# A fused attention and expert kernel: the first piece of weights on two queues, first scores in other banks, another count of filler matmuls

## The chip, the cores and the metric

The kernel runs on one core of a Trainium2 chip. The metric is device microseconds (us) of one execution. A core has TensorE (PE, whose weight loads are shown as PEld), VectorE (DVE), ScalarE (ACT), GpSimd (POOL) and SyncE (SP). Each engine runs its own instructions in order; semaphores tie them together. DMA transfers are issued here by SP and by ACT.

## What is computed

A gated linear recurrence over 4 batches, 8 heads, 768 positions and head dimension 48, whose output is rearranged to 3072 tokens of 384 features and then goes through two dense layers:

```python
for t in range(S):
    state = alpha[:, :, t, :, None] * state + np.einsum('bhd,bhe->bhde', k[:, :, t], v[:, :, t])
    y[:, :, t] = np.einsum('bhd,bhde->bhe', q[:, :, t], state)
...
h = x @ w_in          # 384 -> 2048
g = h - np.tanh(h)
return (g @ w_out).astype(np.float32)
```

q, k, v, alpha are float32; w_in and w_out arrive as 64-bit floats and are converted to 32 bits on the chip.

## The kernel before, in words

The 3072 tokens are cut into 12 units of 256 tokens (2 chunks of 128). For each unit the kernel runs the recurrence in chunked form (`gla`) and then the two dense layers in 8 steps (`moe`), each step a first layer (L1080), elementwise work on ACT and DVE, and a second layer (L1125 for the first two units, L1146 after them). The weights come in 16 pieces, 8 of w_in ("in0" to "in7") and 8 of w_out. A piece is fetched by SP (`fetch`, L551; `load_weight`, L39, whose transfers are all issued at L43), read by ACT in two passes (L86, L87) and written as 32-bit words by DVE in two passes (L89, L90). Four buffers hold raw pieces. A piece of w_in is 8 transfers.

All work is a list of tasks with an engine, an estimated time, a rank, the tasks it needs, and a latency until others see its result. A planner (`Planner`) simulates the list with these estimates several times with other priorities, keeps the shortest plan, and the program is written out in the order of the planned starts: every engine's order follows from the estimates, and the instructions of one engine stay in that order. An estimate itself takes no time on the chip. `plan.begin` (L1210) says from when each engine is counted as free.

The head of the program is unit 0's recurrence. Its path:

- `load` (L576) fetches alpha, k, q, v. For unit 0 each is two transfers, one issued by SP and one by ACT (L584, L595).
- `turn` (L649) transposes alpha, k and q by matmuls with the identity (L663), two halves "a" and "b" each. The halves of alpha go to PSUM banks o0 and o1 and are copied out by ACT and DVE (L670). The halves of q go to the two banks of the tile `sc` (`two_banks`).
- DVE scans the products of alpha (L711, L730), and multiplies the turned k and q by them (L679). For unit 0 the scans and products are made for chunk 0 and chunk 1 apart.
- `scores` (L782): 16 matmuls per chunk (L795). Chunk 0 writes to `two_banks()`, the tile that holds the turned q; chunk 1 writes to two tiles of the pool of `h`. `masked` (L814) multiplies the scores by a mask on DVE (L819).
- `back`, `natural`, `update` (PE L925, ACT L930, PE L938) make the state's update, `products` (L835) the output of a chunk, `features` copies it to xT, and then the first layer can begin.

Behind unit 0's tasks SP issues the loads of unit 1 and the further pieces.

Until the task "y 0.0" (the products of chunk 0) the program puts filler matmuls (`spin`, L1204, 128 x 128 with the identity, result not used) into gaps of PE's plan; each is two matmul instructions in the trace. Their number is counted at L418 with an estimated time each (L1209).

Of the kernel before, what the change touches and what calls it, by code (L numbers as in the profile page):

```python
# [17 lines left out]
P = 128  # L18
# [17 lines left out]
R_MAX = 2.0 ** 60  # L36


def load_weight(nc, pool, rows, **kw):  # L39

    raw = pool.tile([P, WN], I64 if rows[0][2].dtype != FP32 else FP32, name="raw", **kw)
    for at, js, src in rows:
        nc.sync.dma_start(out=raw[at].rearrange("p (j n) -> p j n", n=src.shape[-1])[:, js], in_=src)  # L43
    return raw


def weight_parts(w_in, w_out, pad_rows, what, s, by_tile=True):

    if what == "out":
        return [(slice(0, P), slice(0, 2), w_out.rearrange("(j p) n -> p j n", p=P)[:, 2 * s:2 * s + 2, :])]  # L50
    parts = []
    for i in range(len(pad_rows[0])):
        at, f0 = pad_rows[0][i]
        step = pad_rows[1][i][1] - f0
        src = w_in[f0:f0 + len(pad_rows) * step].rearrange("(j p) n -> p j n", p=step)
        src = src[0:at.stop - at.start, :, 2 * s * P:2 * (s + 1) * P]

        few = at.stop - at.start < 32 or not by_tile
        parts += [(0, at, slice(0, len(pad_rows)), src)] if few else [(j - 9, at, slice(j, j + 1), src[:, j:j + 1]) for j in range(len(pad_rows))]
    return [x[1:] for x in sorted(parts, key=lambda x: (x[0], x[1].start))]  # L60
# [261 lines left out]
class Planner:  # L322
# [64 lines left out]
    def order(self):  # L387
        names = {t[0]: i for i, t in enumerate(self.tasks)}
        assert len(names) == len(self.tasks)
        before, after = ([[] for _ in self.tasks] for _ in range(2))  # L390
        for i, t in enumerate(self.tasks):
            edges = {names[a]: self.tasks[names[a]][6] for a in t[4]}
            if t[7]:
                edges.setdefault(names[t[7]], 0.0 if self.tasks[names[t[7]]][1] == t[1] else 0.25)
            for j, lat in edges.items():
                before[i].append((j, lat))
                after[j].append((i, lat))
        chance = random.Random(self.SEED)
        priority, late, best = [t[3] for t in self.tasks], None, None
        for n in range(self.ROUNDS):  # L400
            starts, order = self.run(priority, before, after, late if n % 2 else None, self.begin)
            ends = [s + t[2] for s, t in zip(starts, self.tasks)]
            if best is None or max(ends) <= best[0]:
                best = max(ends), starts, order
                turned, _ = self.run([-e for e in ends], after, before)
                back = [r + t[2] for r, t in zip(turned, self.tasks)]
                fair = [max(back) - b for b in back]
            late = fair if n < 4 else [x + chance.gauss(0, self.NOISE) for x in fair]
            priority = late
        _, starts, order = best  # L410
        plan = sorted(((starts[i], n, self.tasks[i][5], i) for n, i in enumerate(order)), key=lambda x: x[:2])

        engine, until, us, do = self.filler
        filled, free = [], self.begin.get(engine, 0.0)
        for x in plan:
            name, e, length = self.tasks[x[3]][:3]
            if e == engine and until:
                filled += [(free, -1, do, None)] * int(max(0.0, x[0] - free) / us)  # L418
                free = x[0] + length
                until = until if name != until else None  # L420
            filled.append(x)
        return filled


def fast(tc, q, k, v, alpha, moe_w_in, moe_w_out, out, w_in, w_out, ident, ok, pad_rows):
# [17 lines left out]
    with ExitStack() as ctx:  # L443
# [23 lines left out]
        def by_matmul(u, what):  # L467
            return u < len(TURNED) and what in TURNED[u]
# [80 lines left out]
        raw_of = {}  # L549

        def fetch(what, s):  # L551
            raw_of[what, s] = load_weight(nc, raw_pool, weight_parts(moe_w_in, moe_w_out, pad_rows, what, s), bufs=4)

        def convert(what, s):
            it = []
# [7 lines left out]
        for n, (what, s) in enumerate(pieces):  # L563
            rank = RANK[what] + 2 * s
            held = pieces[n - 4] if n >= 4 else None
            add(f"fetch {what}{s}", "SP", 5.7 if n < 2 else 4.3 if what == "in" else 2.0, rank - 30, [held and f"read {held[0]}{held[1]}"],
                lambda what=what, s=s: fetch(what, s), lat=2.5)
            a, b = convert(what, s)
            older = pieces[n - 2] if n >= 2 else None
            add(f"read {what}{s}", "ACT", 1.9, rank, [f"fetch {what}{s}", older and f"{older[0]}{older[1]}"], a)  # L570
            add(f"{what}{s}", "DVE", 1.6, rank, [f"read {what}{s}"], b)
# [31 lines left out]
        def gla(u, rank):  # L603
# [17 lines left out]
            for what, name in enumerate(("aT", "kT", "qT", "v")):  # L621
                go(f"load {name}", "SP", 1.3 if direct or what == 3 or by_matmul(u, what) else 2.2, -9 + 0.1 * what,
                   [what < 3 and u > 0 and not by_matmul(u - 1, what) and not by_matmul(u, what) and f"{name}{prev}"]
                   + [u == 1 and ("kUba 0" if what == 3 else "turn qTb 0")]
                   + [f"{last} {u - 2}.{CU - 1}" for last in ("y", "state") if what == 3 and u > 1
                      and (last == "y" or (u - 2) % UPB < UPB - 1)],
                   lambda what=what: load(u, what), lat=2.9 if u == 0 else 3.6 if u < PLAIN else 4.5)

            def widen(what):
                for hh in range(2):  # L630
# [51 lines left out]
            for n, ab in enumerate("ab"):  # L682
                if by_matmul(u, 0):
                    go(f"turn aT{ab}", "PE", 0.92, n * 0.1, ["load aT", later and "masked 0.0"], lambda n=n: turn(0, n))
                    go(f"aT{ab}", "DVE" if n else "ACT", 0.62, 0, [f"turn aT{ab}"], lambda n=n: place(n))
                if by_matmul(u, 1):
                    go(f"turn kT{ab}", "PE", 0.92, 1 + n * 0.1,
                       ["load kT"] + [later and x for x in ("x 0.0", "y 0.1", "state 0.1")], lambda n=n: turn(1, n))
                    for x, _, cs in parts:
                        go(f"kU{ab}{x}", "DVE", 0.33 if x else 0.6, 3, [f"turn kT{ab}", f"U{x}", n and f"kUa{x}", later and "back 0.1", later and by_matmul(u, 2) and "turn qTb"],  # L690
                           lambda n=n, cs=cs: times(1, "U", n, cs))
                if by_matmul(u, 2):
                    go(f"turn qT{ab}", "PE", 0.92, 2 + n * 0.1,
                       ["load qT", later and f"aT{ab}" if by_matmul(u, 0) else "masked 0.0"], lambda n=n: turn(2, n))
                    for x, _, cs in parts:
                        go(f"qW{ab}{x}", "DVE", 0.33 if x else 0.6, 5, [f"turn qT{ab}", f"W{x}", n and f"qWa{x}", later and "y 0.1", later and by_matmul(u, 1) and "turn kTb"],
                           lambda n=n, cs=cs: times(2, "W", n, cs))
# [72 lines left out]
            def chunk(c):  # L770
# [11 lines left out]
                def scores():  # L782
                    if c == 0:

                        xT[u] = two.tile([P, NP, TU], FP32, name="xT")
                    if u == 0 and c == 1:
                        sc = m["sc", c] = [ps_h.tile([P, 2, TU], FP32, name="h").rearrange(
                            "p a t -> p (a t)").rearrange("p (g t) -> p g t", t=P) for _ in range(2)]
                    else:
                        m["sc", c] = two_banks()  # L790
                        sc = [m["sc", c][:, r] for r in range(2)]
# [22 lines left out]
                def masked():  # L814
                    sc = m["sc", c]
                    if direct:
                        m["pm", c] = [two.tile([P, NP, P], FP32, name=f"pm{r}", tag=tag) for r, tag in enumerate("zw")]
                        for r, to in enumerate(m["pm", c]):
                            V.tensor_mul(to, sc[r] if c else sc[:, r], mask.unsqueeze(1).to_broadcast([P, NP, P]))  # L819
                        return  # L820
                    of = sc.rearrange("p r g t -> p r (g t)")[:, :, 0:NP * HP].rearrange("p r (g t) -> p r g t", t=HP)
                    V.tensor_mul(pm, of, within.unsqueeze(1).unsqueeze(1).to_broadcast([P, 2, NP, HP]))
# [381 lines left out]
        def spin():  # L1204
# [1 line left out]
            if not spun:  # L1206
                spun.append(ps_o.tile([P, P], FP32, name="spin", tag="o2"))
            T.matmul(spun[0], lhsT=ident, rhs=ident, start=True, stop=True)  # L1208
        plan.filler = "PE", "y 0.0", 0.35, spin  # L1209
        plan.begin.update(SP=0.8, PE=1.5, ACT=3.0, DVE=4.8)  # L1210

        for u in range(NU):
            gla(u, rank_gla(u))
# [108 lines left out]
```

## Time and profile before

| what | value |
|---|---|
| median of 17 runs | 576.24 us (575.63 to 578.96) |
| the profiled execution's own time | 578.32 us |
| its span (first to last instruction) | 576.5 us |
| PE busy, of the span | 565.9 us (98%) |
| DVE busy | 450.8 us (78%) |
| ACT busy | 323.2 us (56%) |
| mean granted TensorE clock | 0.992 |
| first layer's matmuls (L1080), 1152 of them | 265.1 us |
| filler matmuls (L1208) | 38, from 1.57 to 15.6 us |

The profile is of one execution. A line of its timeline gives the start, the duration, the engine, the line of the kernel, the operation, the tiles written and read, and in brackets how long the engine was idle before it and who ended that. Matmuls are pipelined, so busy PE time says little by itself; the waits say where PE stood still.

### The profile page before, as it was taken

The page shows a single profiled execution, that of the slowest core. Times are in us where ns is not written, and L with a number is a line of the kernel's source. Part 1 is how long each engine was busy: PE and PEld are TensorE (multiplying, and loading weights), DVE is VectorE, ACT ScalarE, POOL GpSimd, SP SyncE. Part 2 cuts the span into 40 slices and gives each one's busy share as a digit, 9 for nine tenths or more (in the row PEclk, how much of TensorE's full clock was granted, in tenths as well). Part 3 has the DMA queues.
Part 4 walks back from the last instruction along what each step waited for, and adds up shares of the span by engine and source line. Part 5 has one row for each costly group of instructions (what it writes and reads, how often), then busy time and mean ns, then how long its engine had stood idle before and what let it go on. Part 6 is the DMA issues. An engine that isn't in the chain of part 4 may idle for free.

```text
span 576.5 us, 13746 instructions
## 1 busy us (share of the span) xinstructions
PE 565.9 (98%) x5583; PEld 500.1 (87%) x5583; DVE 450.8 (78%) x886; ACT 323.2 (56%) x559; POOL 4.8 (1%) x22
## 2 busy tenths in 40 slices
PE   8899999999999999999999999999999999999995
PEld 8787777778989998998999999898998999899995
DVE  5889879999999995895896896796797645554643
ACT  2589885747777686577485365364443433333531
POOL 3000000000000000000000000000000000000000
PEclk9799999999999999999999999999999999999999
DMA  8888881236674762562640320210100000000001
GB/s 176 208 227 221 255 183 56 85 71 138 111 154 122 127 156 84 117 148 81 186 116 2 85 60 4 72 53 22 45 20 2 30 7 3 28 8 0 28 1 35
DMA packets 60713, 50.84 MB, mean 88 GB/s; under 512 B 35776, under 2 KB 50400, under 8 KB 60640
## 3 DMA queue, kind: packets, MB, share of 16 engines
q1 hardware_dynamic: 57728, 48.88, 34.4%
q10 hardware_dynamic: 2912, 0.98, 0.8%
q8 instruction: 46, 0.75, 0.6%
q14 instruction: 27, 0.22, 0.1%
HBM read 44.04 MB, written 4.72 MB: 85 GB/s over the span
## 4 chain that ended last, share of the span: by engine, by line
PE 93%; DMA 2%; DVE 2%; SPq 1%; issue 1%; ACT 0%; POOL 0%; DVEq 0%; POOLq 0%
PE h L1080 42%; PE o L1146 32%; PE o L1125 7%; PE sc L805 2%; PE sc L878 2%; PE sc L888 2%; PE sc L811 2%; PE sc L991 1%; DMA raw<-in_moe_w_in_dram 1%; DMA rough<-in_q_dram 1%; PE spin L1208 1%; SPq L43 1%; PE turned L663 0%; DVE W L730 0%; PE sc L795 0%
## 5 line engine op out<-in xcount | busy, mean ns | idle before, releaser
L1080 PE MATMUL h<-xT,w_in 128*128 128x256 f32 x1152 | 265.1, 380 | 0.6 <-DVE w_in L90 0.6
L1080 PEld LDWEIGHTS h<-xT,w_in 128*128 128x128 f32 x1152 | 215.4, 190 | 28.0 <-DVE w_in L90 0.7
L1089 ACT ACTIVATE u<-h 128x512 f32<-128x512 f32 x96 | 57.0, 594 | 179.1 <-PE h L1080 178.4
L1097 DVE TENSOR_TENSOR w<-h,u 128x512 f32<-128x512 f32 x96 | 65.8, 686 | 79.1 <-ACT u L1089 78.7
L1146 PE MATMUL o<-b,e 128*128 128x192 f32 x480 | 90.9, 326 | 0.0
L1146 PE MATMUL o<-w_out,e 128*128 128x192 f32 x320 | 81.4, 337 | 0.0
L1146 PEld LDWEIGHTS o<-b,e 128*128 128x128 f32 x480 | 80.2, 190 | 0.0
L1101 DVE SCALAR_TENSOR_TENSOR g<-z,w 128x512 f32<-128x512 f32 x96 | 65.5, 683 | 4.1 <-PE o L1125 1.3
L1146 PE MATMUL o<-b,g 128*128 128x192 f32 x320 | 65.1, 326 | 0.0
L1093 ACT ACTIVATE z<-u 128x512 f32<-128x512 f32 x96 | 60.4, 629 | 2.6
L1146 PEld LDWEIGHTS o<-w_out,e 128*128 128x128 f32 x320 | 55.7, 189 | 4.4
L1146 PEld LDWEIGHTS o<-b,g 128*128 128x128 f32 x320 | 54.2, 190 | 0.0
L1107 ACT ACTIVATE big<-u 128x1024 f32<-128x1024 f32 x48 | 50.4, 1050 | 0.0
L1125 PE MATMUL o<-w_out,g 128*128 128x384 f32 x128 | 44.0, 488 | 0.0
L1125 PEld LDWEIGHTS o<-w_out,g 128*128 128x128 f32 x128 | 24.1, 190 | 13.7
L1113 DVE TENSOR_TENSOR e<-g 128x256 f32<-128x256 f32 x80 | 33.5, 419 | 1.8
L1114 DVE TENSOR_TENSOR e<-g 128x256 f32<-128x256 f32 x80 | 33.3, 417 | 0.0
L639 DVE STREAM_TRANSPOSE aT<-ar 128x256 f32<-128x256 f32 x44 | 28.4, 645 | 2.8 <-ACT ar L633 1.7
L730 DVE TENSOR_TENSOR_SCAN W<-aT,before 128x1032 f32<-128x1032 f32 (+1 forms) x13 | 27.7, 2133 | 0.0
L711 DVE TENSOR_TENSOR_SCAN U<-aT,after 128x1032 f32<-128x1032 f32 (+1 forms) x13 | 27.6, 2129 | 0.1
L1115 DVE TENSOR_TENSOR e<-g 128x128 f32<-128x128 f32 x80 | 22.7, 284 | 0.0
L639 DVE STREAM_TRANSPOSE qT<-qr 128x256 f32<-128x256 f32 x40 | 20.5, 627 | 0.0
(141 smaller groups left out, 560.4 us busy)
## 6 DMA issues: line engine op xcount, KB each, us to landing
raw<-in_moe_w_out_dram SPq DMA_DIRECT2D x16, 768.0 KB, 4.8
raw<-in_moe_w_in_dram SPq DMA_DIRECT2D x80, 96.0 KB, 4.3
raw<-in_moe_w_in_dram SPq DMA_DIRECT2D x16, 288.0 KB, 4.7
vt<-in_v_dram SPq DMA_DIRECT2D x23, 192.0 KB, 4.1
ar<-in_alpha_dram SPq DMA_DIRECT2D x44, 96.0 KB, 2.5
kr<-in_k_dram SPq DMA_DIRECT2D x40, 96.0 KB, 2.7
qr<-in_q_dram SPq DMA_DIRECT2D x40, 96.0 KB, 2.2
out_dram<-cross SPq DMA_DIRECT2D x19, 96.0 KB, 1.7
```

Source lines behind the costliest of these rows:

```text
L639: V.transpose(to, raws[what][:, g, :, 0:32])
L730: V.tensor_tensor_scan(out=m["W"][:, ns].rearrange("p n t -> p (n t)"), data0=aT[:, a:z], data1=before[:, a:z], initial=0.0, op0=ALU.mult, ...
L1080: T.matmul(h[:, a, :], lhsT=w_in[:, j, f * P:(f + 1) * P], rhs=xT[u][:, j, :], start=(j == 0), stop=(j == KT - 1))
L1089: A.activation(m["u", s], m["h", s], AF.Square, scale=W_SCALE ** -1.5)
L1093: A.activation(m["z", s], m["u", s], AF.Square, bias=QB, scale=QA * W_SCALE)
L1097: V.tensor_mul(m["w", s], m["h", s], m["u", s])
L1101: V.scalar_tensor_tensor(out=g.rearrange("p a c t -> p (a c t)"), in0=m["z", s], scalar=QK, in1=m["w", s], op0=ALU.add, op1=ALU.mult)
L1107: A.activation(big, m["us", s // 2].rearrange("p s t -> p (s t)"), AF.Relu, bias=-U_FAST, scale=W_SCALE, accum_out=over[:, n:n + 1])
L1113: V.tensor_add(e[:, 0:2, :], g[:, 0], g[:, 1])
L1114: V.tensor_sub(e[:, 2:4, :], g[:, :, 1, :], g[:, :, 0, :])
L1125: T.matmul(m["o"][c], lhsT=g[:, a, c, :], rhs=w_out[:, f, :], start=(f == 0), stop=(f == FT - 1))
L1146: T.matmul(o[n][:, i], lhsT=g_, rhs=w_, start=(s_ == 0 and (n, i) in ((0, 0), (1, 0), (2, 1), (3, 0))), stop=(s_ == FS - 1), skip_group_ch ...
```

## The change

- The first piece ("in0") is read over two queues: of its 8 transfers the first, third, fifth and seventh are issued by ACT and the others by SP. `load_weight` gets an argument for it.
- Unit 0's scores of chunk 0 go to tiles in banks o0 and o1 (which held the turned alpha) in place of `two_banks()`. Unit 1's turn of q, which was made to wait for "masked 0.0", is made to wait for unit 0's four qW products in its place.
- A gap of PE's plan gets (gap + 0.5) / 0.24 fillers if it is over 0.2, in place of gap / 0.35.
- Estimates: fetch of the first piece 3.0 in place of 5.7, of the second 5.0 in place of 5.7; latency of unit 0's loads 3.3 in place of 2.9; ACT counted as free from 5.4 in place of 3.0.

```diff
-def load_weight(nc, pool, rows, **kw):
+def load_weight(nc, pool, rows, queues=None, **kw):
...
-    for at, js, src in rows:
-        nc.sync.dma_start(out=raw[at].rearrange("p (j n) -> p j n", n=src.shape[-1])[:, js], in_=src)
+    for n, (at, js, src) in enumerate(rows):
+        (queues[n % len(queues)] if queues else nc.sync).dma_start(out=raw[at].rearrange("p (j n) -> p j n", n=src.shape[-1])[:, js], in_=src)
...
-                filled += [(free, -1, do, None)] * int(max(0.0, x[0] - free) / us)
+                filled += [(free, -1, do, None)] * (int((x[0] - free + 0.5) / us) if x[0] - free > 0.2 else 0)
...
-            raw_of[what, s] = load_weight(nc, raw_pool, weight_parts(moe_w_in, moe_w_out, pad_rows, what, s), bufs=4)
+            raw_of[what, s] = load_weight(nc, raw_pool, weight_parts(moe_w_in, moe_w_out, pad_rows, what, s),
+                                          queues=[A, nc.sync] if (what, s) == pieces[0] else None, bufs=4)
...
-            add(f"fetch {what}{s}", "SP", 5.7 if n < 2 else 4.3 if what == "in" else 2.0, rank - 30, [held and f"read {held[0]}{held[1]}"],
+            add(f"fetch {what}{s}", "SP", 3.0 if n == 0 else 5.0 if n == 1 else 4.3 if what == "in" else 2.0, rank - 30, [held and f"read {held[0]}{held[1]}"],
...
-                   lambda what=what: load(u, what), lat=2.9 if u == 0 else 3.6 if u < PLAIN else 4.5)
+                   lambda what=what: load(u, what), lat=3.3 if u == 0 else 3.6 if u < PLAIN else 4.5)
...
-                       ["load qT", later and f"aT{ab}" if by_matmul(u, 0) else "masked 0.0"], lambda n=n: turn(2, n))
+                       ["load qT"] + [later and f"qW{x}{y} 0" for x in "ab" for y in "ab"], lambda n=n: turn(2, n))
...
-                    if u == 0 and c == 1:
-                        sc = m["sc", c] = [ps_h.tile([P, 2, TU], FP32, name="h").rearrange(
-                            "p a t -> p (a t)").rearrange("p (g t) -> p g t", t=P) for _ in range(2)]
+                    if u == 0:
+
+                        sc = m["sc", c] = [(ps_h if c else ps_o).tile([P, NP, P], FP32, name="scores", tag="h" if c else f"o{r}")
+                                           for r in range(2)]
...
-                            V.tensor_mul(to, sc[r] if c else sc[:, r], mask.unsqueeze(1).to_broadcast([P, NP, P]))
+                            V.tensor_mul(to, sc[r], mask.unsqueeze(1).to_broadcast([P, NP, P]))
...
-        plan.filler = "PE", "y 0.0", 0.35, spin
-        plan.begin.update(SP=0.8, PE=1.5, ACT=3.0, DVE=4.8)
+        plan.filler = "PE", "y 0.0", 0.24, spin
+        plan.begin.update(SP=0.8, PE=1.5, ACT=5.4, DVE=4.8)
```

## The prediction

> **What bounds the kernel now.** I read four views, in this order. First the waits of PE from 30 to 130 us, and the table by stretch (us, then busy us of PE, PEld, DVE, ACT and POOL with their instruction counts, then granted clock, DMA share, GB/s):
>
> ```profile
> PE h L1080 <- DVE w_in L90: 0.6, 1, 0.6
> ```
>
> ```profile
> 120.00:560.00 440.00, 440.00 (x4374) 399.68 (x4373) 343.76 (x689) 235.96 (x421) 0.00 (x0) 1.00 0.28 66
> ```
>
> From 42.8 us on PE never waits: the rest is a fixed amount of TensorE work. So the change, which edits only the head, is worth what it moves the moment at which PE starts to run without a gap. Later pieces of weights follow, since their fetches wait for buffers that the same steps free.
>
> Second, the timeline of the head (start, duration, engine, line; idle time before it and who ended it stand in brackets):
>
> ```profile
> 1.57 4.63 PE L1208 MATMUL spin<-ident 128*128 128x128 f32 x20 [1.57 <-POOL ident masks.py:199]
> 6.13 3.37 PE L663 MATMUL turned<-ident,rough 128*64 128x128 f32 x48
> 7.86 0.64 ACT L670 COPY aT<-turned 128x512 f32<-128x512 f32 x1 [2.84 <-PE turned L663]
> 8.75 0.69 DVE L670 COPY aT<-turned 128x512 f32<-128x512 f32 x1 [3.98 <-PE turned L663]
> 9.55 2.36 DVE L711 TENSOR_TENSOR_SCAN U<-aT,after 128x516 f32<-128x516 f32 x2
> ...
> 12.05 0.94 PE L1208 MATMUL spin<-ident 128*128 128x128 f32 x6
> ...
> 14.70 0.94 PE L1208 MATMUL spin<-ident 128*128 128x128 f32 x6
> ...
> 15.59 0.40 DVE L679 TENSOR_TENSOR qT<-sc,W 128x256 f32<-128x256 f32 x1
> ...
> 17.16 0.42 DVE L679 TENSOR_TENSOR qT<-sc,W 128x256 f32<-128x256 f32 x1
> 17.63 2.08 PE L795 MATMUL sc<-qT,kT 48*128 48x128 f32 x16 [2.00 <-DVE qT L679]
> 19.76 1.29 DVE L819 TENSOR_TENSOR pm<-sc,mask 128x512 f32<-128x512 f32 x2 [2.11 <-PE sc L795]
> 36.63 0.96 DVE L90 CUSTOM_DVE_ANT_0 w_in<-bits,more 128x1536 uint16<-128x1536 uint16 x1 [1.60 <-PE h L1080]
> ```
>
> VectorE is the chain: it runs almost without a gap from the copy at 8.75 to 17.6, idles 2.11 for the first scores, and is full again until the third piece's conversion at 34.5 (L89), whose second half (L90) waits for PE at 36.6. PE's first scores wait for the last of four qT products (17.58), though they use the products of chunk 0 alone, the last of which ends at 15.99: the other two still read the bank (tile sc) that the scores overwrite.
>
> Third, the granted clock (same columns; PEclk after POOL's):
>
> ```profile
> 7.30:17.40 10.10, 8.33 (x126) 7.70 (x122) 8.48 (x18) 5.07 (x10) 0.00 (x0) 1.00 0.79 180
> 17.50:24.30 6.80, 6.67 (x60) 5.77 (x62) 4.48 (x10) 2.88 (x6) 0.00 (x0) 0.50 1.02 227
> 24.40:31.00 6.60, 6.60 (x116) 5.53 (x112) 6.33 (x13) 4.92 (x8) 0.00 (x0) 1.00 0.87 198
> ```
>
> PE was idle from 15.63 to 17.63, and the clock is 0.50 for the next 6.8 us. The early fillers also run slowly (median 421 ns against 275 ns after 12 us) though the column shows 1.00 there; the turns become fast at 7.26.
>
> Fourth, what SP waits for, and how long the two v loads take to land (min/median/max):
>
> ```profile
> SPq L43 <- DMA vt<-in_v_dram: 2.1, 1, 2.1
> SPq L43 <- DMA rough<-in_alpha_dram: 1.7, 1, 1.7
> ```
>
> ```profile
> DMA to landing us min/median/max: 7.1/7.6/8.2
> ```
>
> SP's fifth to twelfth transfers wait for earlier ones to land, in pairs: alpha at 4.6, k at 6.1, q at 7.8, v at 10.7. That is eight transfers in flight, SP's and ScalarE's counted together. So the eight issues of the first piece last from 4.64 to 12.5, most of it waiting.
>
> **Own time and median.** The profiled execution took 578.32 (span 576.5, 1.8 around it); the median shown is 576.24. The difference is about what the half clock costs. Without it the first scores end at 18.7 instead of 19.7, the masks and all of VectorE behind come 1.0 sooner, and L89 ends at 34.0. PE's pieces from 17.63 on, at full speed: scores 1.1, transposes 0.5, scores 1.05, update 0.6, first products 1.75, second products until 25.5 (masks at 22.95), turns 2.75, two first layers 5.4: 33.65. L90 then starts at 34.05, 2.6 sooner, 578.32 - 2.6 = 575.7, close to the lowest shown, 575.63. I take the median as an execution without that stretch.
>
> **Two queues (L43, L552).** SP issues four transfers less; it is free at about 9.9 to 11.1 instead of 12.5, so unit 1's loads and the next pieces go 1.4 to 2.6 sooner. Worth nothing on the path: ScalarE read piece 0 at 15.12 with no wait, piece 1 at 26.13 though it had landed before 21, and the only DMA wait of L86 up to 130 us is 1.3, for a later w_out piece. Those idle-free reads are the cover. The cost is on ScalarE: its four issues stand ahead of the alpha copy (L670), and the last waits for a v load, 9.5 or 10.65, plus 0.4. So the copy can start at 10 to 11.1 instead of 7.86, and the gap copy, sizes and reads queue behind it. With the copy at 11.1 the scan starts at 11.75, 2.2 late; with it at 10, the fillers below decide. The table load (1.28) stands ahead of these issues if the order stays as now; if it falls behind them, see the first rival.
>
> The Trainium skill ("DMA: Bandwidth & Descriptors", Issuing engines are not separate DMA queues) speaks against this part: transfers from several engines interleave on the same 16 DMA engines, and spreading saves only the issue time. Here that time is 0.31 to 0.42 per transfer, so by the rule at most 1.7 is saved on SP; by the waits above up to 2.6; on the path both give 0.
>
> **More fillers (L418, L1209).** Before: (0.8 + 1.3 + 2.9 - 1.5) / 0.35 = 10 ahead of the first turn, the 20 matmuls in the first row. After: latency 3.3, so (3.9 + 0.5) / 0.24 = 18. Ten took 1.57 to 6.0, 0.43 each. Until 7.26 some 13 run; the other 5 at 0.25 end at 8.45. The first turn starts there instead of 6.13, then at 0.875 each (full speed): the second alpha half is ready at 10.25 instead of 8.7. **The scan moves 1.55 later.** The six turns end at 13.7 instead of 12.05. Each of the three later gaps held 3 fillers, so it was 1.05 to 1.4 in the plan; by the new rule 6 (at most 7), 1.5 instead of 0.8. PE: 13.7 + 1.5 = 15.2, transposes 0.44, 1.5, update 0.6, 1.5: free for the scores at **19.2**. With the scan 2.2 late the transposes wait until 15.1, so ScalarE's wait hides under the fillers. What the fillers give: no gap of 2 us, hence no half clock, if that gap was its cause.
>
> The Trainium skill ("TensorE: Matmul & The Clock Gate", HAM oscillation) puts the limit at idle gaps over about 3.4 us. Here 2.0 was enough. By the page the old gap was harmless and the fillers bring nothing; by the row they are worth up to 2.6 in such an execution.
>
> **Banks (L786, L694).** Scores could start at 15.99 + 1.55 = 17.55 on VectorE's side, but PE comes at 19.2: the freed bank is not what ends last any more. Letting unit 1's qT turns go before the masks costs nothing; PE has a queue at 30 us.
>
> **Costs of the plan (5.7 to 3.0 and 5.0, begin 5.4).** They move no instruction by themselves, but the planner may order the head anew. Gain bounded by the only later wait, 0.6; loss by one conversion (1.6) put ahead of masks. I take 0.
>
> **Sum.** Scores 19.2 to 20.3 at full clock; masks at 20.35, 0.6 later than 19.76; L89 ends at 35.65. PE: 20.3 + 0.5 + 1.05 + 0.6 + 1.75 = 24.2, second products until 27.2 (masks 24.6), + 2.75 + 5.4 = 35.35. L90 starts at 35.65, against 36.63: -1.0, so 577.3. Against an execution without the half clock it is 1.6 late: 577.3 too.
>
> **Rivals.**
> - *ScalarE is blocked longer (slower).* Table load and first activation fall behind the four issues: 10.65 + 0.4 + 1.28 + 0.2, copy until 13.2, scan 3.7 late. It decides once the scan is over 2.35 late (transposes at 15.2). Transposes 16.55, scores 20.6 to 21.7, masks 21.75, 2.0 late; L90 at 37.05: +0.4, 578.7. For it: the wait rows, and that the issues of loads already stand ahead of the table load. Against: the first activation was ready at 4.8.
> - *The bank pays in full (faster).* If the clock rises at about 4 or the plan's gaps shrink, scores start at 16.05, masks at 17.65, L89 ends at 32.9, L90 at 32.95: 574.6. For it: the 2.00 wait; against: fillers of 0.43.
> - *Nothing moves.* The stream of weights sets the steady state: 576.2. Against: PE waits 0.6 after 30 us.
>
> **Numbers.** Main case 0.45, its own range 576.6 (the 0.6 gained) to 578.0 (one more filler per gap); blocked ScalarE 0.20; bank 0.22; nothing 0.13. A measurement tells about 0.2% (1.15 us) from no change: bounds 575.1 and 577.4. Half the main case lies above: slower 0.42, within 0.36, faster 0.22. Range 574.5 to 578.9.
>
> **What would show it.** Right: 36 filler matmuls from 1.57 until about 8.4, first turn there, four L43 issues on ACTq ahead of L670, L795 at about 19.2 right behind fillers, clock 1.00 up to the first layer. Wrong: turns starting near 6, L670 after 12, scores before 17, or a half clock again.

## The result and the profile after

| | median | executions |
|---|---|---|
| before | 576.05 us (575.39 to 579.98) | 47 |
| changed | 580.47 us (579.72 to 582.77) | 8 |

The ratio is 1.0072, with a 95% interval of 1.0053 to 1.0091: **slower by 0.7%, 4.4 us, and outside the predicted range.** The profiled execution of the changed kernel took 580.29 (span 578.6, mean granted clock 0.998). Its line numbers are those of the kernel before up to L551, plus 1 from there up to L786 and plus 2 behind it; the other versions shift in the same way by the parts that they hold.

The timeline of the head after the change (start, duration, engine, line; in brackets the idle time before it and who ended it):

```profile
1.57 6.64 PE L1210 MATMUL spin<-ident 128*128 128x128 f32 x36 [1.57 <-POOL ident masks.py:199]
...
6.32 5.75 ACTq L43 DMA_DIRECT2D raw<-in_moe_w_in_dram  x4
8.13 3.71 PE L664 MATMUL turned<-ident,rough 128*64 128x128 f32 x64
...
12.17 0.64 ACT L671 COPY aT<-turned 128x512 f32<-128x512 f32 x1 [7.14 <-DMA raw<-in_moe_w_in_dram]
...
12.84 0.69 DVE L671 COPY aT<-turned 128x512 f32<-128x512 f32 x1 [8.07 <-ACT aT L671]
...
13.63 2.36 DVE L712 TENSOR_TENSOR_SCAN U<-aT,after 128x516 f32<-128x516 f32 x2
...
16.95 0.60 PE L927 MATMUL y<-ident,kT 112*128 112x112 f32 x4 [1.82 <-DVE kT L680]
...
17.39 2.63 PE L1210 MATMUL spin<-ident 128*128 128x128 f32 x22
...
20.55 1.16 PE L797 MATMUL scores<-qT,kT 48*128 48x128 f32 x16
...
21.74 1.29 DVE L821 TENSOR_TENSOR pm<-scores,mask 128x512 f32<-128x512 f32 x2
...
31.86 0.70 PE L1082 MATMUL h<-xT,w_in 128*128 128x256 f32 x2
...
33.27 0.96 DVE L90 CUSTOM_DVE_ANT_0 w_in<-bits,more 128x1536 uint16<-128x1536 uint16 x1
...
34.28 5.02 PE L1082 MATMUL h<-xT,w_in 128*128 128x256 f32 x22 [1.72 <-DVE w_in L90]
```

The fillers are as predicted, 36 until 8.2. But ScalarE's alpha copy runs at 12.17 (7.86 before), VectorE's copy waits for it, and the scan starts at 13.63 (9.55 before). The first scores come at 20.55, the first layer at 31.86, and it stops after two matmuls until the third piece's second conversion (L90, 33.27) is over. The third and the fourth of ScalarE's issues, each from a narrow window of the same timeline, stand just ahead of the late copy; the third waited for a v load that landed at 11.25:

```profile
11.27 0.32 ACTq L43 DMA_DIRECT2D raw<-in_moe_w_in_dram  x1
...
11.63 0.44 ACTq L43 DMA_DIRECT2D raw<-in_moe_w_in_dram  x1
```

TensorE's waits from 6 to 60 us (total, times, longest):

```profile
PE h L1082 <- DVE w_in L90: 2.9, 2, 1.7
...
PE y L927 <- DVE kT L680: 1.8, 1, 1.8
```

Before, the wait for L90 was 0.6. The table by stretch (PE, PEld, DVE, ACT, POOL busy; granted clock, DMA share, GB/s):

```profile
17.50:24.30 6.80, 6.80 (x99) 6.19 (x99) 6.41 (x16) 5.34 (x11) 0.00 (x0) 1.00 0.84 209
...
120.00:560.00 440.00, 440.00 (x4374) 400.08 (x4373) 339.31 (x685) 235.93 (x421) 0.00 (x0) 1.00 0.28 67
```

The steady state is the same (440.00 of 440.00). The half clock of before's profiled execution (0.50 from 17.5 to 24.3) is gone, so this profile hides part of the loss: its span is only 2.1 longer.

One fact is needed for the medians below. Of 130 executions of the kernel before whose clock is recorded, 39 had a mean granted clock of 0.992 or less and a median of 578.5; the other 91 had 0.994 or more and 575.8. An execution with a half clock thus takes about 2.7 longer, and a kernel's median depends on how often it comes. "At full clock" means executions at 0.994 or more.

### The profile page after: what moved, and what is told of

Same layout as the page of the kernel before. It is cut to its first block, busy times and chain, and to the rows that moved or that the text cites. A ratio compares the mean times of both kernels' runs of the same rounds, so it can differ in the third digit from the quotient of the medians.

```text
span 578.6 us, 13800 instructions
## 1 busy us (share of the span) xinstructions
PE 565.7 (98%) x5615; PEld 501.3 (87%) x5615; DVE 450.7 (78%) x886; ACT 322.5 (56%) x559; POOL 4.8 (1%) x22
## 4 chain that ended last, share of the span: by engine, by line
PE 93%; DMA 3%; DVE 2%; issue 1%; ACT 0%; ACTq 0%; DVEq 0%
PE h L1082 43%; PE o L1148 32%; PE o L1127 7%; PE sc L807 2%; PE sc L880 2%; PE sc L890 2%; PE sc L813 2%; PE sc L993 1%; DMA raw<-in_moe_w_in_dram 1%; DMA rough<-in_q_dram 1%; DMA rough<-in_k_dram 1%; DVE U L712 1%; DVE w_in L90 1%; PE spin L1210 0%; PE y L880 0%
## 5 line engine op out<-in xcount | busy, mean ns | idle before, releaser
L1115 DVE TENSOR_TENSOR e<-g 128x256 f32<-128x256 f32 x80 | 33.5, 419 | 1.8
```

The lines of the kernel that those rows point to most:

```text
L1115: V.tensor_add(e[:, 0:2, :], g[:, 0], g[:, 1])
```

## The experiments

Each kernel was compared with the kernel before on the same chip; its median was 575.9 to 576.2 throughout. Diffs are against the kernel before, or against the changed one where the text says so, cut to the lines that matter.

### Each part alone

**queue_only**: only the issue over two queues.

```diff
-def load_weight(nc, pool, rows, **kw):
+def load_weight(nc, pool, rows, queues=None, **kw):
...
+        (queues[n % len(queues)] if queues else nc.sync).dma_start(out=raw[at].rearrange("p (j n) -> p j n", n=src.shape[-1])[:, js], in_=src)
...
+                                          queues=[A, nc.sync] if (what, s) == pieces[0] else None, bufs=4)
```

> The kernel before with only the first piece's transfers split over ScalarE and SP; estimates, order, fillers and banks as before. Theory Q: the alpha copy starts at 11 to 12.2 instead of 7.86, DVE's copy after it, the scan 3 to 4 late, of which the idle 2.1 of DVE hides nothing: about 579 to 579.5. Theory P: the order is unchanged, so 576 to 576.5.

582.59 (580.13 to 584.05), ratio 1.0096 [1.0067, 1.0126]. More than expected. Its timeline, and the clock:

```profile
6.01 6.18 ACTq L43 DMA_DIRECT2D raw<-in_moe_w_in_dram  x4
...
12.29 0.62 ACT L671 COPY aT<-turned 128x512 f32<-128x512 f32 x1 [7.26 <-DMA raw<-in_moe_w_in_dram]
...
17.06 1.01 PE L926 MATMUL y<-ident,kT 112*128 112x112 f32 x4 [5.05 <-DVE kT L680]
```

```profile
17.50:24.30 6.80, 6.80 (x62) 6.00 (x62) 5.37 (x14) 3.60 (x8) 0.00 (x0) 0.66 0.99 233
```

The copy is as late as in the changed kernel. Without the added fillers TensorE idles 5.05 for the late scan and the half clock comes (5 of 6 executions at 0.992 or less). Delay and half clock together are the +6.5; the one execution at 0.995 took 580.1, so the delay alone is about 4.3 of it, by a single execution.

**plan_only**: only the four estimates.

```diff
-            add(f"fetch {what}{s}", "SP", 5.7 if n < 2 else 4.3 if what == "in" else 2.0, rank - 30, [held and f"read {held[0]}{held[1]}"],
+            add(f"fetch {what}{s}", "SP", 3.0 if n == 0 else 5.0 if n == 1 else 4.3 if what == "in" else 2.0, rank - 30, [held and f"read {held[0]}{held[1]}"],
...
-                   lambda what=what: load(u, what), lat=2.9 if u == 0 else 3.6 if u < PLAIN else 4.5)
+                   lambda what=what: load(u, what), lat=3.3 if u == 0 else 3.6 if u < PLAIN else 4.5)
...
-        plan.begin.update(SP=0.8, PE=1.5, ACT=3.0, DVE=4.8)
+        plan.begin.update(SP=0.8, PE=1.5, ACT=5.4, DVE=4.8)
```

> The kernel before with only the four estimates changed (3.0, 5.0, latency 3.3, ScalarE free from 5.4), so only the planned order moves (and 11 fillers instead of 10 ahead of the first turn). Theory P: conversions of w_in stand ahead of the first layers that do not need them, PE waits 2 to 3 for them behind 30 us: 578 to 578.5. Theory Q: 576 to 576.5.

579.47 (577.42 to 581.04), ratio 1.0046 [1.0028, 1.0064]. The estimates are not free. They reorder the head: SP fetches the second piece ahead of unit 1's alpha, and VectorE converts the third piece from 31.9 to 33.5, just as the first layer begins (31.97); before, L90 of that piece stood at 36.6. TensorE waits 0.9 and 1.2 for L90:

```profile
31.97 0.70 PE L1080 MATMUL h<-xT,w_in 128*128 128x256 f32 x2
...
32.58 0.96 DVE L90 CUSTOM_DVE_ANT_0 w_in<-bits,more 128x1536 uint16<-128x1536 uint16 x1
...
33.59 5.02 PE L1080 MATMUL h<-xT,w_in 128*128 128x256 f32 x22 [0.93 <-DVE w_in L90]
```

Nine of 12 executions were at 0.993 or less; the three others had a median of 578.4, so at full clock the order costs 2.6.

**bank_only**: only the new banks of the first scores.

```diff
+                        sc = m["sc", c] = [(ps_h if c else ps_o).tile([P, NP, P], FP32, name="scores", tag="h" if c else f"o{r}")
...
+                       ["load qT"] + [later and f"qW{x}{y} 0" for x in "ab" for y in "ab"], lambda n=n: turn(2, n))
```

> The kernel before with only unit 0's first scores in the banks that alpha left and unit 1's turn of q waiting for the qW products. Both theories: scores start at 16.05 instead of 17.63, the gap of PE shrinks from 2.0 to about 0.4 and the half clock does not follow, masks at 17.65: 574.6 to 575.0, and no execution near 578. If the bank were not what ended last, 576.05 as before.

575.18 (573.96 to 578.24), ratio 0.9979 [0.9958, 0.9999]: faster, though by less than expected, and two executions took 577.9 and 578.2 at full clock, which is not explained.

```profile
15.04 1.16 PE L796 MATMUL scores<-qT,kT 48*128 48x128 f32 x16 [0.41 <-DVE qT L679]
```

The wait of 2.00 is 0.41, and no execution of 12 had a clock under 0.996. What ends last then was not separated. TensorE waits 1.6 in all for L90, in three pieces, and ScalarE's reads of the weights, which L90 follows, wait for transfers; its waits from 30 to 120 us:

```profile
ACT more L86 <- DMA raw<-in_moe_w_in_dram: 2.9, 2, 1.7
...
ACT more L86 <- DMA raw<-in_moe_w_out_dram: 2.5, 2, 2.1
```

**fill_only**: only the count of fillers.

```diff
-                filled += [(free, -1, do, None)] * int(max(0.0, x[0] - free) / us)
+                filled += [(free, -1, do, None)] * (int((x[0] - free + 0.5) / us) if x[0] - free > 0.2 else 0)
...
-        plan.filler = "PE", "y 0.0", 0.35, spin
+        plan.filler = "PE", "y 0.0", 0.24, spin
```

> The kernel before with only the filler rule changed: 16 ahead of the first turn and 6 in each of three gaps, order as before. Theory of the prediction: first turn near 8.0, first scores near 18.7 right behind fillers, no half clock: 577.2, and no execution above 578.3. Rival: the fillers hide in gaps that PE had anyway and only save the half clock: 575.8 with no execution above 577.

577.15 (576.47 to 579.87), ratio 1.0013 [0.9995, 1.0031]: the median as expected, but one execution took 579.87, over the 578.3 that was named. Scan at 10.25, scores at 18.33, no wait ahead of them, no half clock. The fillers give and take: the median is 1.3 above before's executions at full clock (575.8), but the ratio, which counts those with a half clock too, shows no clear loss.

### Two parts, and the change without one

**bank_fill**: banks and fillers, SP alone, old estimates (the two diffs above together).

> The kernel before with the bank and the fillers, SP alone, old estimates. Theory (with the fillers in place TensorE comes to the scores last, so the freed bank gives nothing more): within 0.5 of the fillers alone, 576.8 to 577.5. Rival (the two effects add: +1.0 and -0.9): 576.2. If it lands at 578 or above, fillers and bank together have a cost that the two runs alone do not show.

577.2 (576.33 to 577.77), ratio 1.0004 [0.9987, 1.0021]: the theory. As with the fillers alone, the loss stands in the medians and against full clock (1.4), and not in the ratio. VectorE's masks now wait for TensorE's scores, which stand right behind fillers:

```profile
17.36 1.60 PE L1209 MATMUL spin<-ident 128*128 128x128 f32 x12
...
18.90 1.16 PE L796 MATMUL scores<-qT,kT 48*128 48x128 f32 x16
...
20.09 1.29 DVE L820 TENSOR_TENSOR pm<-scores,mask 128x512 f32<-128x512 f32 x2 [1.00 <-PE scores L796]
```

**sp_only**: the changed kernel with all transfers issued by SP (the diff of queue_only undone).

> The changed kernel with all eight transfers of the first piece issued by SP again; estimates, banks and fillers as changed, so the planned order is that of the changed kernel. Theory Q (ScalarE's in-order issue, which held the alpha copies until 12.17 and 12.84, is the main cost): the copies come right behind the turns, the scan starts near 11.1 instead of 13.63, and the time falls by about 2.5, to near 578. Theory P (the new order, with PE waiting 1.7 and 1.2 for conversions in w_in that it does not read, is the main cost): the head comes earlier but the waits grow by as much; 579.5 or more.

578.55 (577.73 to 579.46), ratio 1.0026 [1.001, 1.0041]. Scan at 11.34, scores at 18.82, both about 2 earlier than in the changed kernel, and the time is 1.9 shorter. The waits for L90 are those of the changed kernel, 2.9 in all.

```profile
9.65 0.65 ACT L670 COPY aT<-turned 128x512 f32<-128x512 f32 x1 [4.62 <-PE turned L663]
...
11.34 2.36 DVE L711 TENSOR_TENSOR_SCAN U<-aT,after 128x516 f32<-128x516 f32 x2
...
18.82 1.16 PE L796 MATMUL scores<-qT,kT 48*128 48x128 f32 x16
```

**old_plan**: the changed kernel with the estimates of before (the diff of plan_only undone).

> The changed kernel with the four estimates of before, so queues, banks and fillers as changed in the order of before. Theory: the two waits for L90 of 2.9 in all shrink to the 0.6 of before, ScalarE's queue still holds the scan until about 13.6: 578 to 578.3. If the new order were no cost of its own, 580.5.

579.69 (579.2 to 583.39), ratio 1.0062 [1.0038, 1.0085]. Only 0.8 under the changed kernel, less than expected. The copy is at 12.08 all the same and the scan at 13.55, so the head is as late. The waits for L90 fall to 1.4, not to 0.6, and TensorE waits 2.5 for kT. That a late head leaves the order less to spoil is a reading of this, not shown.

**after_two**: ScalarE issues the first and third transfer only.

```diff
-        (queues[n % len(queues)] if queues else nc.sync).dma_start(out=raw[at].rearrange("p (j n) -> p j n", n=src.shape[-1])[:, js], in_=src)
+        (queues[n % len(queues)] if queues and n < 4 else nc.sync).dma_start(out=raw[at].rearrange("p (j n) -> p j n", n=src.shape[-1])[:, js], in_=src)
```

> The changed kernel, but ScalarE issues only the first and the third of the first piece's transfers; SP issues the other six. Theory (not the number of issues but the wait of the last ones for the v loads, 11.25 and 11.63, holds up ScalarE's in-order queue): those two issues wait for the k and q loads only (6.3 and 7.9), so ScalarE's alpha copy starts right behind the turns and fillers (near 9.5 to 10.5), the scan near 11.2 to 11.5, and the kernel is at the time of the version with SP alone, 578.5. Rival (any issue on ScalarE costs, for its own length or because the piece's transfers collide with the loads): copy after 11.5 and 579.5 to 580.5, as the changed kernel.

578.5 (577.74 to 580.15), ratio 1.0035 [1.0018, 1.0052]: the time of sp_only.

```profile
6.29 1.89 ACTq L43 DMA_DIRECT2D raw<-in_moe_w_in_dram  x2
...
8.91 0.64 ACT L671 COPY aT<-turned 128x512 f32<-128x512 f32 x1 [3.89 <-PE turned L664]
...
10.60 2.36 DVE L712 TENSOR_TENSOR_SCAN U<-aT,after 128x516 f32<-128x516 f32 x2
```

The copy waits for the turns again. By the times, two issues on ScalarE that wait for k and q cost nothing, and the two behind a v load are the whole price. The path is not that of sp_only, though: TensorE waits 1.4 for L90 in place of 2.9, and 0.6 for unit 1's k.

### The late copy, and the waits for L90

**after_dve_copy**: the changed kernel with both alpha copies on VectorE.

```diff
-                (V.tensor_copy if n else A.copy)(gc(tail[:, :, 0:P]).rearrange("p g c (i two) -> p g c i two", two=2)[:, :, :, :, n],
+                V.tensor_copy(gc(tail[:, :, 0:P]).rearrange("p g c (i two) -> p g c i two", two=2)[:, :, :, :, n],
...
-                    go(f"aT{ab}", "DVE" if n else "ACT", 0.62, 0, [f"turn aT{ab}"], lambda n=n: place(n))
+                    go(f"aT{ab}", "DVE", 0.62, 0, [f"turn aT{ab}"], lambda n=n: place(n))
```

> The changed kernel with both alpha copies on DVE, so that nothing on the path stands behind ScalarE's four issues. Theory Q (ScalarE's queue costs through the alpha copy alone): copies at about 9.6 and 10.4, scan at 11.2 instead of 13.63, as with SP alone: 578.5. If the split costs by contention of the transfers instead (the loads land later), the scan stays at 12.5 or later and the time at 580.

579.4 (578.54 to 580.4), ratio 1.004 [1.0022, 1.0058]. A miss by 0.9. The scan started 3.4 sooner (10.20), but the copy kn (L932) stood in ScalarE's queue behind the read of the first piece, which landed at 16.3 here:

```profile
PE y L940 <- ACT kn L932: 1.6, 1, 1.6
```

**after_layout**: the changed kernel, w_in laid out so that a piece is one stretch of a partition. Before, each partition held three stretches per piece, with other pieces' stretches between them.

```diff
-    w_in = consts.tile([P, KT, d_ff], FP32, name="w_in")
+    w_in = consts.tile([P, FT // 2, KT, 2 * P], FP32, name="w_in")
...
-                dst = w_in[:, :, 2 * s * P:2 * (s + 1) * P] if what == "in" else w_out[:, 2 * s:2 * s + 2, :]
+                dst = w_in[:, s] if what == "in" else w_out[:, 2 * s:2 * s + 2, :]
...
-                            T.matmul(h[:, a, :], lhsT=w_in[:, j, f * P:(f + 1) * P], rhs=xT[u][:, j, :],
+                            T.matmul(h[:, a, :], lhsT=w_in[:, s, j, a * P:(a + 1) * P], rhs=xT[u][:, j, :],
```

> The changed kernel with the converted w_in laid out piece by piece (each piece one stretch of every partition), so that the regions of two pieces no longer interleave; order, fillers, banks and queues as changed. Theory F (PE's waits of 1.7 and 1.2 for L90 are for the conversion of a later piece, made only because the regions interleave): both waits go, about 2.3 to 2.9 less: 577.6 to 578.2. Theory D (PE waits for data it reads): 580.5, the waits stay.

579.29 (578.34 to 581.41), ratio 1.0046 [1.0025, 1.0068]: -1.2, where more was expected.

```profile
31.86 5.45 PE L1082 MATMUL h<-xT,w_in 128*128 128x256 f32 x24
...
38.02 0.99 PE L993 MATMUL y<-ident,kT 112*128 112x112 f32 x8 [0.71 <-DVE kT L680]
```

The order and the conversion at 33.27 are the same, yet the 24 matmuls run through it: they do not read what it writes. The wait was **false**, made by the layout. The next true wait, 0.71 for kT, takes back part.

**plan_layout**: the four estimates alone, with this layout.

> The four estimates with w_in laid out in one stretch per piece. Theory (the first layer's waits of 0.93 and 1.21 for L90 are false and carry most of the cost of the estimates): 577.4 to 578.3, 1.2 to 2.1 under the estimates alone (579.47). Rival (a later wait, kT of unit 1, is as late): 579.2 to 579.6.

577.63 (576.24 to 580.42), ratio 1.0022 [1.0001, 1.0044]. -1.8 against plan_only by medians; by full clock 577.4 against 578.4 (nine and three executions). Part of that drop is fewer half clocks (3 of 12 in place of 9). The false waits are a good part of what the estimates cost, not all.

**before_layout**: the kernel before with this layout.

> The kernel before, with w_in laid out so that each piece is one stretch of a partition. Theory (the first layer's waits for L90, and L90's wait of 1.6 for the first layer, are between regions that do not overlap but lie interleaved): these waits go, TensorE gets 0.6 or a little more: 575.2 to 575.6. Rival (something else ends at the same place, such as kT for the next unit, or the stream of weights): 576.0 with the waits moved to other names.

575.35 (574.78 to 579.11), ratio 0.9994 [0.9973, 1.0015]: the median fell as expected, and at full clock it is 575.1 against 575.8, but the interval does not show a gain.

**est_fetch**: the kernel before with the two fetch estimates only.

```diff
-            add(f"fetch {what}{s}", "SP", 5.7 if n < 2 else 4.3 if what == "in" else 2.0, rank - 30, [held and f"read {held[0]}{held[1]}"],
+            add(f"fetch {what}{s}", "SP", 3.0 if n == 0 else 5.0 if n == 1 else 4.3 if what == "in" else 2.0, rank - 30, [held and f"read {held[0]}{held[1]}"],
```

> The kernel before with only the two fetch estimates (3.0 and 5.0). It loads q before k, puts the second piece's fetch behind unit 1's alpha as before, and both masks ahead of the first conversion. Theory (the fetch estimates are what brings the second and third conversions forward, and so the whole cost of the estimates): 578.5 to 579.5, as all four. Rival (each single estimate gives some other order, good or bad by chance): 575.5 to 577.

579.92 (575.39 to 581.93), ratio 1.0042 [1.0012, 1.0073]. The number is the theory's, the reason is not: the two executions at a clock of 0.998 took 575.4 and 576.0. The other seven took 579.1 to 581.9, six of them at 0.989 or 0.990 and one at 0.994, too few to say more. This order makes TensorE idle 2.77 ahead of the scores:

```profile
17.45 2.08 PE L795 MATMUL sc<-qT,kT 48*128 48x128 f32 x16 [2.77 <-DVE qT L679]
```

```profile
17.50:24.30 6.80, 6.80 (x46) 5.82 (x48) 2.79 (x6) 3.37 (x9) 0.00 (x0) 0.50 0.82 205
```

**est_lat**: the kernel before with the latency only.

```diff
-                   lambda what=what: load(u, what), lat=2.9 if u == 0 else 3.6 if u < PLAIN else 4.5)
+                   lambda what=what: load(u, what), lat=3.3 if u == 0 else 3.6 if u < PLAIN else 4.5)
```

> The kernel before with only the loads' latency 3.3. One filler more ahead of the first turn (+0.25 to 0.4 on the path), and the first piece's conversion (0.55 and 0.96) goes into VectorE's idle 2.11 ahead of the first masks; SP's order is the same. Theory (order of fetches and later conversions makes the cost, and this estimate leaves it): 576.0 to 576.6. Rival (the latency is what costs): 578 or more.

575.39 (574.27 to 578.98), ratio 0.9996 [0.9975, 1.0017]: costs nothing, less even than the 576.0 to 576.6 expected; the first piece's conversion fits ahead of the masks. So neither the fetches nor the latency carries the cost by itself, and the rival fits better: every set of estimates gives an order of its own. ScalarE's 5.4 was not run alone.

### A version without the costs

**best**: the freed bank and the new layout, all else as before.

> The freed bank and the contiguous layout, with the fillers, queue and estimates of before. Theory (the freed bank moves VectorE's chain 1 to 2 earlier, and the waits for L90 took back part of it): 574.0 to 574.6, about 0.6 under the bank alone (575.18). Rival (the waits for L90 were hidden behind a later one): 575.2, as the bank alone.

576.11 (574.06 to 576.95), ratio 0.9986 [0.9968, 1.0004]. A miss: 0.9 above the bank alone, at full clock throughout. The two intervals overlap; why it isn't faster stays open.

**best7**: the same with at most 7 fillers in a gap, so 7 and not 10 ahead of the first turn.

```diff
-                filled += [(free, -1, do, None)] * int(max(0.0, x[0] - free) / us)
+                filled += [(free, -1, do, None)] * min(7, int(max(0.0, x[0] - free) / us))
```

> Freed bank, contiguous layout, and 7 fillers ahead of the first turn in place of 10. Theory (the stream of weights through ScalarE and VectorE now ends last: first layers wait for L90 at 53.5 and 64.7): the head gets 0.5 to 0.8 earlier and the time stays, 575.0 to 576.2. Rival (the head still sets it): 0.5 to 0.8 below the same kernel with 10 fillers, 574.0 to 575.3.

574.47 (573.86 to 576.94), ratio 0.9975 [0.9959, 0.9992]: faster than both kernels, the opposite of the theory that the weights alone set the time. Scan at 8.60, first layer at 26.63 without a wait:

```profile
26.63 5.45 PE L1081 MATMUL h<-xT,w_in 128*128 128x256 f32 x24
...
29.03 1.08 ACT L86 ACTIVATE more<-raw 128x768 int16<-128x768 uint32 x1 [2.06 <-DMA raw<-in_moe_w_in_dram]
```

ScalarE already waits 2.06 for the third piece here, so the stream of weights is close behind. Best7 has 0.4 of idle ahead of its scores, like bank_only, and like it no half clock in 12 executions.

## Why the prediction was wrong

The terms can be laid end to end from the medians:

| kernel | median | step |
|---|---|---|
| before | 576.05 | |
| + banks and fillers (bank_fill) | 577.2 | +1.15 |
| + estimates (sp_only) | 578.55 | +1.35 |
| + ScalarE's four issues (changed) | 580.47 | +1.9 |

The runs stand on several chips, where the kernel before differs by up to 0.3, so a step is no surer than that. In the other order ScalarE's issues come to +2.5 (579.69 against 577.2) and the estimates to +0.8: both delay the same chain, so a share of the cost belongs to neither alone. The sum of the prediction, 577.3, is the time of the first two parts. The two parts costed at 0 were not 0.

- **Fillers: right.** 18 ahead of the first turn, which starts at 8.13 (8.45 predicted). The sum of 577.3 is met by bank_fill's 577.2 (with 16 fillers there), and so are its terms: scores at 18.90 (19.2), masks at 20.09 (20.35), the third piece's L90 at 35.93 (35.65).
- **Banks: right, with its rival.** "the freed bank is not what ends last any more" is what bank_fill shows. Alone it gave 0.9, where the rival in which it pays in full went to 574.6.
- **Half clock: right.** A stretch was priced at 2.6; the two groups of executions of before are 2.7 apart.
- **Two queues: the failed step is "With the copy at 11.1 the scan starts at 11.75, 2.2 late", and "ScalarE's wait hides under the fillers".** Its own views had the mechanism (issues that wait for v loads ahead of the copy) and a rival with its threshold: it decides "once the scan is over 2.35 late". The scan was 4.08 late, and TensorE waited 1.82 for what follows it, until 16.95 (15.1 in the prediction). Three things were missed. The v load that the third issue waits for landed at 11.25, not 10.65 (why wasn't separated). The fourth issue stood behind the third (11.63). And VectorE's copy did not run at 10.25 beside it but behind ScalarE's copy (12.84), so 0.69 more came on the path. The rival (578.7) was the nearer one, but it took the table load for its reason, which did not move, and without the changed estimates the case took 579.7 (old_plan).
- **SP "free at about 9.9 to 11.1": no gain.** SP's four issues were over at 7.8, but in the estimates' new order it went straight on with the second piece, whose first issue (10.98) came ahead of the first piece's last (11.63, on ScalarE). By the trace the first piece was complete at 15.79, 14.71 before. In queue_only, with the old order, unit 1's first load was issued at 10.67 in place of 12.54, as forecast, and landed at 14.96 in place of 15.02.
- **Estimates: the failed step is "They move no instruction by themselves ... I take 0".** The bounds set there, -0.6 and +1.6, were worked out from the order of before. The new order put another conversion ahead of the first layer, and its waits (2.9 in place of 0.6) are between regions that do not overlap. Which estimate does it isn't settled: the latency alone costs nothing, the fetches alone nothing in the two executions at 0.998 (575.4 and 576.0), and ScalarE's 5.4 alone was not run.

The Trainium skill ("DMA: Bandwidth & Descriptors", Issuing engines are not separate DMA queues) says that issuing from more engines saves only issue time. The runs agree that there is nothing more to gain: after_two and sp_only are 578.5 and 578.55. That four issues lose 1.9 is what the runs add.

## What to carry to other kernels

A DMA issue with a wait is a wait of the engine that issues it: ask what its last issue waits for, and put no such issue on an engine ahead of work on the path (two issues cost nothing here, the next two 1.9). In a planned program a changed estimate is a changed order, to be costed by reading the new order engine by engine, not by the estimate's size. Where a wait is for a write that the reader doesn't read, look at the layout of the tile: one contiguous stretch per piece removed waits of 1.7 and 1.2.

## What the runs showed of the hardware

- **A half clock came after waits of about 2, by chance, and the length of the wait alone does not decide it.** Kernels with no wait ahead of the scores, or 0.4 (fill_only, bank_fill, sp_only, after_two, bank_only, best, best7), had no execution of 84 at 0.993 or less. With 2.0 it was 39 of 130 (before) and 4 of 12 (before_layout), with 1.7 1 of 12 (est_lat), with 2.77 6 of 9 (est_fetch), with 5.05 5 of 6 (queue_only). In plan_only, with two waits of 1.17 and 0.77 close together, it was 9 of 12, in plan_layout, with one of 2.6, 3 of 12. But the kernels with the added fillers and a late head waited 1.6 (after_dve_copy), 1.8 (the changed kernel) and 2.5 (after_layout, old_plan) and had 2 of 45. Some half clock may hide there: three executions each of the changed kernel and old_plan, at 0.993 to 0.995, took 581.4 to 583.4, 2 to 3 above the median of the others. What makes the difference was not tried. The added fillers did keep the clock up in fill_only; at the median there was little to win by it, since most executions of before have no half clock.
- The Trainium skill ("TensorE: Matmul & The Clock Gate", HAM oscillation) sets the limit at gaps of over about 3.4 us; the half clocks after a wait of 2.0 (39 of 130) decide against it for this kernel.
- **Fillers took from 1.57 to 8.51 in one profiled execution (sp_only) and to 7.78 in another (after_two), 36 each.** They start every 0.21 us at first and every 0.11 later; the step comes at 7.07 in the one and at 5.57 in the other, and moves the start of the turns by 0.7. Where profiles of two versions are compared, so much of a difference in the head can be chance.
- **A second issuing engine did not bring a piece sooner**: the first piece's last transfer landed at 15.79 (changed) and 15.89 (queue_only), against 14.71 (before) and 14.06 (sp_only) with SP alone.
- **Two copies on two engines into interleaved halves of one tile ran one behind the other** (12.17 and 12.84) when both were ready: VectorE's was released by ScalarE's. Whether other halves would let them overlap was not tried.
